# Attention and FFN on one core: later batches in five steps of three score units, three rotating PSUM bank pairs, and a last third of the FFN weights that VectorE holds back

## The chip, the cores and the metric

One core of one Trainium2 chip. The metric is the device time of one execution in microseconds (us); lower is better. A time is the median over the runs of a kernel; each experiment ran in five rounds beside the kernel before, on the same chip. A difference of less than 2% counts as "the same". In the profiles PE is TensorE, ACT ScalarE, DVE VectorE, POOL GpSimd and SP SyncE; L498 is line 498 of the kernel of that profile, so line numbers differ by a few between kernels.

## The reference

Causal attention for 8 batches of 8 heads with 576 queries and 16 "beacon" keys ahead of the 576 keys, then a gated FFN over all 4608 rows:

```python
def _attn_ref(q, k, v, beacon_k, beacon_v):
    B, H, S, D = q.shape                      # 8, 8, 576, 64
    k_all = np.concatenate([beacon_k, k], axis=2)
    v_all = np.concatenate([beacon_v, v], axis=2)
    scores = (1.0 / np.sqrt(D)) * np.matmul(q, k_all.transpose(0, 1, 3, 2))
    ...                                       # causal mask, softmax over the keys
    return np.matmul(a, v_all)

def _moe_ref(x, w_gate, w_val, w_out):        # x: 4608 x 512, FFN width 1536
    gate = np.maximum(x @ w_gate, 0.0)
    return (gate * (x @ w_val)) @ w_out
```

Inputs and outputs are float32; the kernel computes in bf16 with float32 sums.

## The kernel before

The program is written as a list of steps. A step of attention takes two score units (a unit fills up to a pair of PSUM banks with scores), their exponentials on ACT, causal masks on POOL, the weighted sums ("values") of an earlier chunk of queries, and then some FFN products of rows that are finished. Batch 0 and 1 go in an order of their own; batches 2 to 7 are the *later batches*, seven steps of two units each. The FFN of one tile of 512 rows is 12 *slices* (a gate product, its Relu on ACT, a value product, their product hT on DVE) and four *down* products of 12 matmuls.

The eight PSUM banks belong to three pools: two pairs for scores, two banks for FFN products, one each for the values and their row sums.

```python
s_ps = main.enter_context(tc.tile_pool(name="s_ps", bufs=2, space=bass.MemoryType.PSUM))
o_ps = main.enter_context(tc.tile_pool(name="o_ps", bufs=1, space=bass.MemoryType.PSUM))
f_ps = main.enter_context(tc.tile_pool(name="f_ps", bufs=2, space=bass.MemoryType.PSUM))
# ... cut ...
def up(self, nf, c0, c1, spare):                       # one slice
    # ...
    g = f_ps.tile([P, M_TILE], FP32, name="f")          # gate product into g
    # ... 4 matmuls; gs = Relu(g) on ScalarE
    if spare:
        u = s_ps.tile([P, 2, M_TILE], FP32, name="s")[:, 0]
    else:
        u = f_ps.tile([P, M_TILE], FP32, name="f")      # value product into u
    # ... 4 matmuls; hT = gs * u on VectorE
```

The front, that is the work on batches 0 and 1, loads everything that comes later: on POOL's queue the third part of the gate and value weights ("thirds", four loads of 192 KB as the profile counts them) and the output weights (wo, two loads), on SP's queue the tiles of q, k and v, which POOL casts to bf16 and SP then transposes.

```python
for t in range(NKT):
    after(7, lambda t=t: second.load("v", t, t == 0))
for t in range(NKT):
    after(s2 - 1 + t // 2, lambda t=t: second.cast("v", t, pool))
after(s2 - 2, lambda: load_w(wg, moe_w_gate, 1152, 1536))     # thirds
after(s2 - 2, lambda: load_w(wv, moe_w_val, 1152, 1536))
after(s2 - 1, lambda: load_wo(0, 6))                          # output weights
after(s2, lambda: load_wo(6, 12))
# ... cut ...
def fetch(b, s0, late=1):
    for j, u in enumerate(UNITS):                 # k, q, v of tile 0, then of tile 1, ...
        s = s0 + j // 3                           # three loads a step
        at(s, lambda u=u: batches[b].load(*u))
        at(s + late, lambda u=u: batches[b].cast(*u, pool))
        if u[0] != "v":
            at(s + late + 1, lambda u=u: batches[b].turn(*u))   # transpose on SP

fetch(2, s2, 3)
fetch(3, BASE[3] - STEPS - 2, 2)
for b in range(4, B):
    fetch(b, BASE[b] - STEPS)
```

## Time and profile before

| what | value |
|---|---|
| median of 3 runs | 393.25 us (390.98 to 393.74) |
| span of the profiled run | 389.1 us |
| PE busy | 374.1 us, 96% |
| DVE, ACT, POOL busy | 53%, 50%, 33% |
| one later batch (same product to same product) | 40.55 us |
| idle of PE, all waits | 10.0 us, all before 120 us |

The profile of a kernel is read from the bound engine outward: the busy shares and the row of slices say which engine and which stretch matter, the timeline of that engine says what one period costs, and its list of waits says who ended each pause. PE's last pause, and one period, from a down product to the same one of the next batch:

```profile
118.73 0.29 PE L368 MATMUL s<-qT,kT 64*128 64x128 bf16 x4 [0.28 <-DMA qT<-half]
...
146.67 5.35 PE L483 MATMUL f<-wo,hT 128*128 128x512 bf16 x24
...
187.22 5.35 PE L483 MATMUL f<-wo,hT 128*128 128x512 bf16 x24
```

PE shows no pause from 120 us on, so there only PE's own work counts. Before that it pauses for 10.0 us in all, and there what counts is who comes late.

### The profile page before, as it was taken

What the parts mean: (1) busy time and instruction counts of PE and PEld (TensorE: products, weight loads), DVE (VectorE), ACT (ScalarE), POOL (GpSimd) and SP (SyncE); (2) the same over time, 40 slices, a digit from 0 to 9 for tenths busy, and PEclk for the clock granted to TensorE, in tenths of its full rate; (3) what the DMA queues carried; (4) which work ended last, traced back from release to release, by engine and by line L of the source; (5) the groups of instructions that cost most, each with busy time, mean ns of one, the idle gap of its engine ahead of it and who ended that gap; (6) DMA issues with size and microseconds to landing.
All of it is one profiled execution on the core that took longest, in us unless ns stands there. A gap on an engine that the chain in (4) does not pass through costs nothing.

```text
span 389.1 us, 10272 instructions
## 1 busy us (share of the span) xinstructions
PE 374.1 (96%) x4297; PEld 187.4 (48%) x4297; DVE 204.3 (53%) x342; ACT 192.9 (50%) x270; POOL 127.8 (33%) x220
## 2 busy tenths in 40 slices
PE   7889889998999999999999999999999999999995
PEld 3554435543554545545544545445545454444443
DVE  4767456543566566465547653757266635512420
ACT  4763556336555554565546554655466533323321
POOL 1597284334462462253414351435021100000000
PEclk9999989999999999999999999999999999999999
DMA  8999999979996996499449933993300020011002
GB/s 215 215 186 178 200 199 210 166 174 174 215 161 164 188 183 125 115 203 172 101 128 193 182 86 106 197 203 77 98 29 2 2 83 29 0 52 59 0 29 87
DMA packets 148132, 50.44 MB, mean 130 GB/s; under 512 B 133616, under 2 KB 143600, under 8 KB 148080
## 3 DMA queue, kind: packets, MB, share of 16 engines
q1 hardware_dynamic: 139024, 44.48, 57.2%
q0 software_dynamic: 9056, 5.24, 9.8%
q8 instruction: 35, 0.57, 0.7%
q14 instruction: 17, 0.14, 0.1%
HBM read 38.34 MB, written 9.44 MB: 123 GB/s over the span
## 4 chain that ended last, share of the span: by engine, by line
PE 75%; DMA 12%; SPq 6%; POOL 4%; issue 1%; DVE 1%; ACT 0%; POOLq 0%; DVEq 0%
PE f L483 22%; PE f L464 21%; PE s L473 11%; PE f L473 9%; PE ab L418 6%; PE s L368 5%; DMA raw<-in_v_dram 5%; DMA raw<-in_k_dram 2%; PE os L418 2%; SPq L244 2%; DMA wv<-in_moe_w_val_dram 2%; SPq L268 2%; SPq L281 1%; DMA qT<-half 1%; POOL e L384 1%
## 5 line engine op out<-in xcount | busy, mean ns | idle before, releaser
L376 ACT ACTIVATE e<-s 128x1024 bf16<-128x1024 f32 (+2 forms) x112 | 104.9, 963 | 25.3 <-PE s L368 25.3
L464 PE MATMUL f<-xT,wg 128*128 128x512 bf16 x432 | 112.2, 382 | 0.3 <-DMA hwide<-in_k_dram 0.3
L467 ACT ACTIVATE g<-f 128x512 f32<-128x512 f32 x108 | 64.5, 597 | 84.6 <-PE f L464 82.6
L483 PE MATMUL f<-wo,hT 128*128 128x512 bf16 (+1 forms) x444 | 96.7, 374 | 0.0
L384 POOL TENSOR_SCALAR_AFFINE_SELECT e<-e 128x512 bf16<-128x512 bf16 (+2 forms) x80 | 46.8, 597 | 135.6 <-ACT e L376 127.6
L430 DVE RECIPROCAL r<-os 128x80 f32<-128x80 f32 (+2 forms) x43 | 57.6, 1339 | 57.0 <-PE os L418 57.0
L475 DVE TENSOR_TENSOR hT<-g,s 128x512 bf16<-128x512 f32 x60 | 41.2, 687 | 66.4 <-PE s L473 65.3
L473 PEld LDWEIGHTS <-wv 128*128 128x128 bf16 x432 | 42.3, 98 | 53.3 <-issue 3.0
L483 PEld LDWEIGHTS <-hT 128*128 128x128 bf16 x444 | 41.9, 98 | 47.3
L464 PEld LDWEIGHTS <-wg 128*128 128x128 bf16 x432 | 39.6, 98 | 46.8 <-issue 1.7
L473 PE MATMUL s<-xT,wv 128*128 128x512 bf16 x240 | 61.6, 379 | 0.0
L486 ACT COPY ob<-f 128x512 f32<-128x512 f32 (+1 forms) x37 | 21.3, 575 | 73.9 <-PE f L483 71.9
L475 DVE TENSOR_TENSOR hT<-g,f 128x512 bf16<-128x512 f32 x48 | 33.0, 688 | 36.6 <-PE f L473 32.0
L473 PE MATMUL f<-xT,wv 128*128 128x512 bf16 x192 | 49.8, 381 | 0.6 <-DMA wv<-in_moe_w_val_dram 0.4
L263 POOL CAST half<-raw 128x512 bf16<-128x512 f32 (+2 forms) x60 | 37.4, 634 | 31.0 <-DMA raw<-in_k_dram 11.3
L418 PE MATMUL ab<-e,v 128*32 128x80 bf16 (+4 forms) x1320 | 39.3, 233 | 3.8 <-POOL e L384 3.8
L368 PE MATMUL s<-qT,kT 64*128 64x80 bf16 (+3 forms) x704 | 35.8, 235 | 1.8 <-ACT e L376 1.0
L418 PEld LDWEIGHTS <-v 128*32 128x32 bf16 (+1 forms) x1408 | 26.5, 97 | 13.6 <-issue 9.0
L259 POOL CAST v<-raw 128x512 bf16<-128x512 f32 (+1 forms) x40 | 26.5, 664 | 19.3 <-DMA raw<-in_v_dram 19.3
L368 PEld LDWEIGHTS <-kT 64*128 64x128 bf16 x704 | 20.3, 96 | 25.8 <-issue 23.7
L418 PE MATMUL os<-e,ones 128*32 128x240 bf16 (+4 forms) x660 | 32.2, 232 | 0.0
L443 DVE TENSOR_TENSOR xT<-ab,r 128x480 bf16<-128x480 f32 (+2 forms) x45 | 24.9, 554 | 0.8
(66 smaller groups left out, 134.7 us busy)
## 6 DMA issues: line engine op xcount, KB each, us to landing
out_dram<-ob SPq DMA_DIRECT2D x35, 256.0 KB, 2.1
raw<-in_q_dram SPq DMA_DIRECT2D x25, 256.0 KB, 4.8
raw<-in_v_dram SPq DMA_DIRECT2D x24, 256.0 KB, 5.0
raw<-in_k_dram SPq DMA_DIRECT2D x19, 256.0 KB, 4.3
raw<-in_v_dram SPq DMA_DIRECT2D x8, 224.0 KB, 4.2
wo<-in_moe_w_out_dram POOLq DMA_DIRECT2D x2, 768.0 KB, 9.9
raw<-in_k_dram SPq DMA_DIRECT2D x6, 224.0 KB, 4.5
raw<-in_v_dram SPq DMA_DIRECT2D x8, 160.0 KB, 4.3
```

What stands on the lines that cost most here:

```text
L259: copy(self.v[:n, t].rearrange("p (h a d) -> p h a d", a=2, d=C), raw[:n].rearrange("p (h d a) -> p h a d", a=2, d=C))
L263: copy(h[:n], raw[:n])
L368: nc.tensor.matmul(self.s[:, a, c + j * n:c + (j + 1) * n], kT[rows, 2 * g + j, k0:k0 + P], qT[rows, 2 * g + j, q0:q0 + n], start=True, st ...
L376: nc.scalar.activation(e[:, :k * 4 * n].rearrange("p (k a x) -> p a k x", k=k, a=2), self.s[:, :, :k * 2 * n].rearrange("p a (k x) -> p a ...
L384: nc.gpsimd.affine_select(out=cols[:, :, :m], in_=cols[:, :, :m], pattern=[[0, 4], [1, m]], compare_op=ALU.is_ge, fill=0.0, base=base, cha ...
L418: nc.tensor.matmul(o[:, q0 - cq0:q0 - cq0 + n], w, e[:kr, 2 * (hh % 2) + hh // 2], start=(i == 0 and part != 1), stop=(i == self.last), sk ...
L430: nc.vector.reciprocal(self.r[:, :n], self.os[:, :n])
L464: nc.tensor.matmul(g[:, :n], wg[:, ki, nf * P:(nf + 1) * P], x[:, ki], start=(ki == 0), stop=(ki == KM - 1))
L467: nc.scalar.activation(gs[:, :n], g[:, :n], AF.Relu)
L473: nc.tensor.matmul(u[:, :n], wv[:, ki, nf * P:(nf + 1) * P], x[:, ki], start=(ki == 0), stop=(ki == KM - 1))
L475: nc.vector.tensor_mul(self.h[:, nf, c0:c1], gs[:, :n], u[:, :n])
L483: nc.tensor.matmul(o[:, n], self.h[:, nf, ms * P:(ms + 1) * P], wo[:, nf, n], start=(nf == 0), stop=(nf == NF - 1))
```

## The change

The intent: every change of tile shape on PE costs about 0.1 us, so fewer and larger steps (five steps of 3, 3, 3, 3 and 2 units) save some. Three units at a time need three pairs of score banks, so the two score pairs and the two FFN banks become three pairs in one rotation, and FFN products use one bank of a pair. Chunks 0 and 2 of a head group are summed in one go. In the front, DVE writes one element of the last weight third after an FFN product; the load of that third has to wait for it, so that the v tiles of batch 1 get the DMA engines first.

```diff
+SHARES_FIRST, SHARES = (2,) * 7, (3, 3, 3, 3, 2)
-    s_ps = main.enter_context(tc.tile_pool(name="s_ps", bufs=2, ...PSUM))
-    f_ps = main.enter_context(tc.tile_pool(name="f_ps", bufs=2, ...PSUM))
+    # s_ps and f_ps are closed when batch 2 starts, then:
+            pools["p"] = main.enter_context(
+                tc.tile_pool(name="p_ps", bufs=3, space=bass.MemoryType.PSUM))
+    LOADS = ([("k", 0), ("q", 1), ("k", 1), ("q", 2), ("k", 2), ("q", 3), ("k", 3), ("q", 0),
+              ("k", 4), ("q", 4)] + [("v", t) for t in range(NKT)])
+    def bank():
+        return pair()[:, 0] if "p" in pools else f_ps.tile([P, 512], FP32, name="f")
...
-            g = f_ps.tile([P, M_TILE], FP32, name="f")
+            g = bank()
...
-                u = f_ps.tile([P, M_TILE], FP32, name="f")
+                u = bank()
...
+        def load_thirds():
+            nc.vector.memset(wg[:1, 0, 1152:1153], 0.0)
+            load_w(wg, moe_w_gate, 1152, 1536)
+            load_w(wv, moe_w_val, 1152, 1536)
+            for t in range(2, NKT):
+                second.load("v", t, t == 2)
+        after(s2 - 1, load_thirds)
+        # load_wo(0, 6) and load_wo(6, 12) both after(s2, ...), behind the casts of v 0 and 1
...
-        fetch(2, s2, 3)
-        fetch(3, BASE[3] - STEPS - 2, 2)
-        for b in range(4, B):
-            fetch(b, BASE[b] - STEPS)
+        fetch(2, s2 + 1, 2, True)
+        for b in range(3, B):
+            fetch(b, BASE[b] - 5)          # and fetch() goes through LOADS, not UNITS
...
             for j, u in enumerate(units):
-                u.qk()
+                if len(units) > 2 and not chunks and j == 0:
+                    u.qk(o_ps.tile([P, 2, 512], FP32, name="o"))
+                else:
+                    u.qk()
...
+            if len(units) > 2:
+                for u in units[1:]:
+                    u.exp()
```

The cuts: the new order of units, the sums of two chunks in one tile, the wider tiles for their reciprocals, and bookkeeping.

## The prediction

> **What bounds the kernel now.** I read the page's busy shares and slices first, then the table of stretches, then TensorE's (PE) timeline through one later batch, with ScalarE's (ACT) and VectorE's (DVE) beside it, and last PE's waits.
>
> ```profile
> PE 374.1 (96%) x4297; PEld 187.4 (48%) x4297; DVE 204.3 (53%) x342; ACT 192.9 (50%) x270; POOL 127.8 (33%) x220
> ...
> PE   7889889998999999999999999999999999999995
> ...
> PEclk9999989999999999999999999999999999999999
> ```
>
> PE is busy 96%, every other engine about half. From the stretches (start:end, length, busy us and count of each engine):
>
> ```profile
> 40.00:60.00 20.00, 16.95 (x194) 8.20 (x193) 10.55 (x13) 11.80 (x17) 9.72 (x17) 0.91 1.16 200
> ...
> 80.00:100.00 20.00, 18.67 (x134) 8.54 (x133) 8.88 (x14) 10.87 (x15) 7.44 (x13) 1.00 0.88 171
> ...
> 160.00:180.00 20.00, 20.00 (x211) 9.79 (x196) 12.65 (x19) 12.21 (x17) 9.17 (x16) 1.00 1.05 180
> ...
> 200.00:220.00 20.00, 20.00 (x246) 10.03 (x241) 12.19 (x18) 12.77 (x18) 8.59 (x16) 1.00 1.00 184
> ```
>
> From 120 us until the last matmuls PE has no idle time. The same down projection starts at 146.67, 187.22 and 227.77 in the PE timeline: 40.55 us a batch. So from 120 us on only PE's own time counts; before that PE idles about 10 us. One step of a later batch, by start and length (the length contains the drain, so the next start is what counts):
>
> ```profile
> 162.76 1.03 PE L473 MATMUL f<-xT,wv 128*128 128x512 bf16 x4
> 163.72 0.61 PE L368 MATMUL s<-qT,kT 64*128 64x256 bf16 x8
> 164.26 0.39 PE L418 MATMUL ab<-e,v 128*32 128x240 bf16 x8
> 164.47 0.28 PE L418 MATMUL os<-e,ones 128*32 128x240 bf16 x4
> 164.58 0.28 PE L418 MATMUL ab<-e,v 128*32 128x128 bf16 x8
> 164.69 0.23 PE L418 MATMUL os<-e,ones 128*32 128x128 bf16 x4
> 164.85 1.04 PE L464 MATMUL f<-xT,wg 128*128 128x512 bf16 x4
> 165.72 1.03 PE L473 MATMUL f<-xT,wv 128*128 128x512 bf16 x4
> ```
>
> Four 512-column matmuls take 0.86 to 0.87 us (164.85 to 165.72). The group before the scores takes 0.96 (162.76 to 163.72): 0.10 more. Eight score matmuls (two at a time, 1024 columns each, 0.43 us at 2.4 columns per ns) take 0.54: 0.11 more. The values (4416 columns, four at a time, 0.46 us) take 0.59: 0.13 more. So a step with values pays 0.34 us for three changes of tile shape; one without values pays 0.10 + 0.11 = 0.21.
>
> Two stalls lie in the front, both on POOL's masks, the first followed by a half-speed gate product (1.68 us to the next start, against 0.86):
>
> ```profile
> 50.22 0.39 PE L418 MATMUL ab<-e,v 128*32 128x240 bf16 x8 [2.15 <-POOL e L384]
> 50.42 0.29 PE L418 MATMUL os<-e,ones 128*32 128x240 bf16 x4
> 51.00 0.41 PE L418 MATMUL ab<-e,v 128*32 128x128 bf16 x8 [0.29 <-POOL e L384]
> 51.17 0.35 PE L418 MATMUL os<-e,ones 128*32 128x128 bf16 x4
> 51.45 0.61 PE L368 MATMUL s<-qT,kT 64*128 64x256 bf16 x4
> 51.99 1.89 PE L464 MATMUL f<-xT,wg 128*128 128x512 bf16 x4
> ```
>
> The other is 1.33 us at 95.03, for the same reason.
>
> **What the Trainium skill says.** "TensorEngine Tiling (Array Packing)", Tiling Modes, Key Properties: changing the tiling mode, not just the tile, drains TensorE. The trace agrees: 0.10 to 0.13 us at each change. "TensorE: Matmul & The Clock Gate", Part 1: after an idle window of some 3.4 us the array clock falls to half until a busy window passes. The trace agrees in size (1.68 against 0.86) though the idle before it was only 2.15 + 0.29 us in one piece and more. "PSUM — Partial Sum Buffer", Specifications: eight banks of 512 fp32 per partition. Both kernels use all eight, before as 2 x 2 for scores, 2 for FFN products and 2 for values, after as 3 pairs plus one pair. "DMA: Bandwidth & Descriptors", Issuing engines are not separate DMA queues: all transfers share 16 engines. The trace agrees: from 52 to 56 us POOL's queue moved 0.59 MB and SP's 0.12 MB, and an SP load issued there took 11.4 us to land.
>
> **The change part by part.** The order of instructions of the changed kernel has the same matmuls, but 36 fewer stretches of one tile shape: 12 fewer each of scores, values and FFN.
>
> 1. *Fewer steps: gain.* A later batch goes from six steps with values and one without (6 x 0.34 + 0.21 = 2.25 us) to four and one (1.57): 0.68 us a batch, 4.1 us for six batches.
>
> 2. *Three rotating pairs: new waits.* Each score unit, gate, value or down product now takes the next of three pairs, so each waits for the reader of the third product before it. Before, FFN products rotated in their own banks, and PE never waited. Durations from the rows: exp of 1024 columns 1.02 us, a second follows 0.93 after the first; relu 0.60; hT product 0.69; output copy 0.59. Reader starts after PE's last issue: exp 0.22 (170.14 + 0.21 to 170.57), hT product 0.27 (170.31 against 170.04), copy 0.21. I take 0.06 us from a reader's end to PE's next start. Counted from the end of the FFN before:
> - Step 0 (two downs before it): its third unit needs the pair of the second down, copied at 0.21 + 0.59 + 0.06 = 0.86. PE is there at 0.10 + 0.21 + 0.21 = 0.52. Wait 0.34.
> - Step 1 (no values, first unit in the values' pair): the first value product needs the pair of the second unit. The first exp, behind the copy, starts at 0.69, the second ends at 0.69 + 0.93 + 0.97 = 2.59, PE may go at 2.65. PE arrives at 0.10 + 0.61 (three units) + 0.11 + 0.86 = 1.68. Wait 0.97.
> - Step 2: its third unit needs the pair of the last value product, free at 0.27 + 0.69 + 0.06 = 1.02; PE is there at 0.10 + 0.13 + 0.21 = 0.44. Wait 0.58.
> - Step 3: the same with 0.52 for 0.44. Wait 0.50.
> - Step 4 has two units and no such wait.
>
> Sum 2.39 us a batch against 0.68 gained: +1.7 us a batch, a period of 42.25 us. Five batches (3 to 7): +8.5 us. Batch 2 has short steps: waits of about 0.8, 0.2, 0.6, 0.6, 0.5 and 0.3 (values waiting for DVE's scaling), 3.0 - 0.7 = +2.3 us.
>
> 3. *Merged chunks.* One 320-column reciprocal replaces one of 240 and one of 80: 2.16 us (line through 657 ns at 80 and 1758 at 256) for 2.31, and fewer minimum and maximum instructions. DVE is 53% busy; nothing on the path.
>
> 4. *New unit order and load order for batch 2 on.* The 1.33 us stall near 95 us and a 0.28 us one at 118.73 go, because values come two steps after their masks: -1.6 us.
>
> 5. *Last weight third held, wo later.* The memset sits in DVE's order behind an hT product that ends near 44.5 us. POOL waits there, issues four loads (0.71 us each) to 47.5, casts two v tiles to 48.8, masks at 49.35: the values start at 49.4 instead of 50.22, their second part at 50.0 instead of 51.0, and with only 1.3 us idle the half clock (about 1.2 us lost) should not come: some 2 us gained by 54 us. But both halves of wo are now issued behind those masks, at 50.5 to 52.3 instead of 48.7 and 52.6, into engines that still carry the thirds. At 0.15 MB per us (0.59 MB in 4 us) the 1.57 MB run from 53 to 63.5 or 64; the second half is needed 1.3 us into the first down, at about 61.5. That is 2 to 2.5 us of wait. SP's loads creep meanwhile, and POOL stands at batch 2's casts ahead of masks that batch 1 needs: 1 to 2 us more, perhaps a half clock. Net of the front: +2 us, uncertain by 2.5.
>
> Sum: 8.5 + 2.3 - 1.6 + 2 = +11.2 us if all holds. I shade it to +9.75, since the front is the weakest part and small waits can overlap: 403.0 us.
>
> **The rivals.** (a) *The switches decide*: the waits of part 2 hide, PE stays full, 4.1 us of drains and 1.6 + 2 us of front go: about 385.5 us. For it: PE has shown no wait in 270 us. Against: in step 1 two exps of about 1 us each must end before a product that PE reaches in 1.68 us; and in the built program that product's pair is the second unit's. (b) *Drains and waits cancel*: if the consumers start sooner than I read, waits of 1.0 a batch leave 0.3 us a batch, and the front decides: 392 to 396 us. (c) *A longer front*: the wo wait brings the half clock and batch 3's loads, now spread over only five short steps, come late: 408 us. For it: DMA was above 0.9 busy in the slices to 120 us. (d) *DVE becomes the bound* through the 2.16 us reciprocal: it would delay the first hT product of a step; against it, the pair it holds is needed only three products later.
>
> **Range and chances.** The steady part is +8.5 + 2.3 with perhaps 2 us of error, the front -2 to +5. So 403.0 us, 8 in 10 within 396 to 409. Slower by 2% begins at 401.1 us: 0.64 for slower, 0.31 for within 2%, 0.05 for faster.
>
> **What would show it.** In the changed profile: the starts of the same down 42.2 us apart in batches 4 to 6 (40.55 before); PE waiting for the score exps (about 1 us, once a batch), for hT (about 0.5, twice) and for the output copy (0.3, once); PE below 20.0 in 20 us in the stretches after 120; about 0.34 us per step of drains as before; the values of batch 1 starting near 49.4 us; a PE wait for wo near 62 us; no wait for POOL near 95. A period under 40.5 us would prove part 2 wrong; PE full again from 120 us on would prove rival (a); no wait at the first down would prove part 5 wrong.

## More of the kernel before

The experiments ran in four groups (e1 to e4, e5 to e8, e9 to e11, e12), each on another chip, so across groups the ratios are compared, not the times.

## The result, and the profile after

The changed kernel took 406.41 us (405.55 to 407.61, four runs) against 392.75 us (four runs) for the kernel before beside it: ratio 1.0355, 95% interval 1.0307 to 1.0402, slower. A ratio here is the mean time of one kernel's fast runs over the mean of the other's fast runs of the same rounds, so it is not quite the ratio of the medians.

The page of the changed kernel, busy time and slices:

```profile
PE 369.7 (91%) x4252; PEld 189.0 (47%) x4297; DVE 198.6 (49%) x307; ACT 191.3 (47%) x270; POOL 124.2 (31%) x222
...
PE   6879787899896999989998999999999999999995
...
PEclk9799998999999999999999999999999999999999
```

The span is 404.7 us for 389.1. PE's busy time reads lower than before (369.7 for 374.1), but 45 of its 4297 matmul records are missing from this trace (x4252; e10, with all of them, has 375.4), so that is no gain. In the later batches four matmuls still take 0.86 to 0.87 us (173.38 to 174.25 below): they did not get slower, PE waits. In the stretches (start:end, length, then busy time and number of each engine, PE first) it is no longer at 20.00 in the later batches:

```profile
160.00:180.00 20.00, 18.86 (x202) 9.31 (x203) 6.50 (x10) 10.10 (x15) 6.46 (x12) 1.00 0.68 161
```

Whom PE waited for (sum, times, longest):

```profile
PE p L381 <- DVE hT L500: 4.6, 13, 0.5
PE p L498 <- ACT e L389: 4.3, 5, 1.0
PE o L438 <- POOL e L397: 3.6, 3, 1.4
PE p L381 <- DMA qT<-half: 3.1, 1, 3.1
PE f L508 <- DMA wo<-in_moe_w_out_dram: 2.5, 1, 2.5
```

The tile `p` is a rotating pair. The first two lines are the later batches, the other three the front and batch 3. All waits of PE sum to 27.7 us (some of the missing records count as pauses in it), against 10.0 before. One later batch in PE's timeline (start, length, operation, number; in brackets the pause shown ahead of it and who ended it):

```profile
170.85 0.40 PE L381 MATMUL o<-qT,kT 64*128 64x128 bf16 x8
...
171.60 0.82 PE L489 MATMUL p<-xT,wg 128*128 128x512 bf16 x3
173.38 1.02 PE L498 MATMUL p<-xT,wv 128*128 128x512 bf16 x4 [0.96 <-ACT e L389]
174.25 1.02 PE L489 MATMUL p<-xT,wg 128*128 128x512 bf16 x4
...
179.52 0.54 PE L381 MATMUL p<-qT,kT 64*128 64x80 bf16 x12
180.43 0.39 PE L381 MATMUL p<-qT,kT 64*128 64x256 bf16 x4 [0.38 <-DVE hT L500]
...
182.02 1.04 PE L489 MATMUL p<-xT,wg 128*128 128x512 bf16 x3
...
215.47 1.02 PE L498 MATMUL p<-xT,wv 128*128 128x512 bf16 x4 [0.96 <-ACT e L389]
```

From 173.38 to 215.47 a batch takes 42.09 us, where it took 40.55. In step 1 (170.85) a value product waits until an exponential has read the pair that it is to fill; ACT's timeline shows which:

```profile
171.44 1.03 ACT L389 ACTIVATE e<-o 128x1024 bf16<-128x1024 f32 x1
172.35 1.84 ACT L389 ACTIVATE e<-p 128x960 bf16<-128x960 f32 x2
```

The first exponential reads the output pair, which PE does not need back for a whole step; the one PE waits for stands second. In step 2 (179.52) the third unit waits for the hT product that reads its pair. Two warnings on the brackets. The group at 171.60 has three records of four: one matmul is missing from the trace, so the 0.96 holds the missing 0.21 or so as well; where all four records are there (several experiments below) the same wait reads 0.74. And the 0.38 is too small, since the end of a matmul is a modelled time: the Trainium skill, "Perfetto Trace Analysis", Tensor Engine Instruction, says that the profiler estimates a matmul's end from its size. The starts tell more, and they are used further down.

The front and batch 3 in PE's timeline:

```profile
53.23 0.60 PE L498 MATMUL f<-xT,wv 128*128 128x512 bf16 x2 [0.66 <-DMA wv<-in_moe_w_val_dram]
...
66.33 2.04 PE L508 MATMUL f<-wo,hT 128*128 128x512 bf16 x6 [2.54 <-DMA wo<-in_moe_w_out_dram]
...
130.10 0.39 PE L381 MATMUL p<-qT,kT 64*128 64x80 bf16 x12 [3.08 <-DMA qT<-half]
...
131.29 1.03 PE L498 MATMUL p<-xT,wv 128*128 128x512 bf16 x4
```

POOL's timeline around the write of DVE that holds the thirds back:

```profile
45.67 1.41 POOL L341 DMA_DIRECT2D wg<-in_moe_w_gate_dram  x2 [7.49 <-DVE wg L693]
...
51.41 1.67 POOL L359 DMA_DIRECT2D wo<-in_moe_w_out_dram  x2
```

POOL stands 7.49 us at DVE's write, issues the thirds, and the output weights only at 51.41. The thirds are then late for the products that need them (0.66, and 0.80 at 54.63), the output weights 2.54 us late for the first down product; the six matmuls behind that wait take 2.04 us at reduced clock (0.91 of full in the stretch from 60 to 80 us), where six take 1.46 or 1.47 in other runs. At 79.31 a mask is 1.18 us late. The last down product ahead of batch 2 starts at 79.75, against 73.75 before. In batch 3 the transpose of the last q tile comes 3.08 us late (130.10); it was issued only in that batch's own step 0.

Where the 15.6 us between the two profiled runs lie: 6.0 before the last down product of the front, of which 1.4 were there at the first FFN product (27.99 us against 26.56); the experiments have that product at 26.7 to 28.4, so these 1.4 are the run's. Five later batches of +1.54 make 7.7. Batch 3's late transpose adds 2.35, not the whole 3.08: behind it the first value product of step 1 waits for no exponential any more (131.29), and from step 1 to the next batch's step 1 are 44.44 us (126.41 to 170.85) where the other later batches take 42.09. That is 16.05; batch 2 and the end give back 0.45.

### The profile page after: what moved, and what is told of

Read it like the earlier page. It is cut to its first block, busy times and chain, and to the rows that moved or that the text cites. A ratio compares the mean times of both kernels' runs of the same rounds, so it can differ in the third digit from the quotient of the medians.

```text
span 404.7 us, 10190 instructions
## 1 busy us (share of the span) xinstructions
PE 369.7 (91%) x4252; PEld 189.0 (47%) x4297; DVE 198.6 (49%) x307; ACT 191.3 (47%) x270; POOL 124.2 (31%) x222
## 4 chain that ended last, share of the span: by engine, by line
PE 69%; DMA 10%; SPq 7%; ACT 4%; issue 3%; DVE 3%; POOL 3%; DVEq 0%; ACTq 0%; POOLq 0%
PE p L498 18%; PE p L508 18%; PE p L489 17%; PE o L438 6%; SPq L247 3%; DMA raw<-in_v_dram 3%; PE f L489 2%; DMA raw<-in_k_dram 2%; DVE hT L500 2%; PE p L381 2%; ACT e L389 2%; DMA wv<-in_moe_w_val_dram 2%; PE s L498 1%; SPq L271 1%; ACT ob L511 1%
## 5 line engine op out<-in xcount | busy, mean ns | idle before, releaser
L500 DVE TENSOR_TENSOR hT<-g,p 128x512 bf16<-128x512 f32 x89 | 60.9, 684 | 108.5 <-PE p L498 79.6
L498 PE MATMUL p<-xT,wv 128*128 128x512 bf16 x355 | 91.3, 379 | 4.4 <-ACT e L389 4.3
L492 ACT ACTIVATE g<-p 128x512 f32<-128x512 f32 x89 | 53.3, 599 | 80.2 <-PE p L489 78.5
L489 PE MATMUL p<-xT,wg 128*128 128x512 bf16 x335 | 89.4, 379 | 0.9
L508 PE MATMUL p<-wo,hT 128*128 128x512 bf16 (+1 forms) x383 | 84.6, 373 | 0.8 <-issue 0.2
L451 DVE RECIPROCAL r<-o 128x256 f32<-128x256 f32 (+3 forms) x31 | 55.8, 1799 | 54.4 <-PE o L438 54.4
L389 ACT ACTIVATE e<-p 128x1024 bf16<-128x1024 f32 (+2 forms) x77 | 68.9, 961 | 12.6 <-PE p L381 12.6
L438 PE MATMUL o<-e,v 128*32 128x80 bf16 (+4 forms) x1320 | 38.4, 234 | 4.3 <-POOL e L397 3.6
L389 ACT ACTIVATE e<-s 128x1024 bf16<-128x1024 f32 (+2 forms) x28 | 25.7, 962 | 8.7 <-PE s L381 8.7
L489 PE MATMUL f<-xT,wg 128*128 128x512 bf16 x73 | 19.5, 380 | 0.5 <-DMA hwide<-in_k_dram 0.3
```

The source lines that it names most:

```text
L389: nc.scalar.activation(e[:, :k * 4 * n].rearrange("p (k a x) -> p a k x", k=k, a=2), self.s[:, :, :k * 2 * n].rearrange("p a (k x) -> p a ...
L438: nc.tensor.matmul(o[:, q0 - cq0:q0 - cq0 + n], w, e[:kr, 2 * (hh % 2) + hh // 2], start=(x == 0 and i == 0 and part != 1), stop=stop, ski ...
L451: nc.vector.reciprocal(self.r[:, :self.n], self.os[:, :self.n])
L489: nc.tensor.matmul(g[:, :n], wg[:, ki, nf * P:(nf + 1) * P], x[:, ki], start=(ki == 0), stop=(ki == KM - 1))
L492: nc.scalar.activation(gs[:, :n], g[:, :n], AF.Relu)
L498: nc.tensor.matmul(u[:, :n], wv[:, ki, nf * P:(nf + 1) * P], x[:, ki], start=(ki == 0), stop=(ki == KM - 1))
```

## The experiments

All outputs are right.

| label | edit, in a few words | time, us | ratio to before | 95% interval |
|---|---|---|---|---|
| (changed kernel) | | 406.41 | 1.0355 | 1.0307 to 1.0402 |
| e1_pair_shared | gate and value product share a pair | 486.12 | 1.2433 | 1.2389 to 1.2476 |
| e2_third_late | third unit behind the values | 402.33 | 1.0269 | 1.0243 to 1.0294 |
| e3_old_front | old loads, new order of batch 2's tiles | 410.58 | 1.0495 | 1.0467 to 1.0523 |
| e4_front_only | kernel before with the new front | 395.13 | 1.0092 | 1.0070 to 1.0114 |
| e5_third_in_o | third unit in the output pair | 405.57 | 1.0364 | 1.0320 to 1.0409 |
| e6_batch3_earlier | batch 3 fetched earlier | 404.20 | 1.0326 | 1.0280 to 1.0371 |
| e7_early_hold | DVE's write earlier | 405.47 | 1.0337 | 1.0302 to 1.0373 |
| e8_all_four | e2, e5, e6 and e7 together | 395.26 | 1.0066 | 1.0037 to 1.0096 |
| e9_whole_old_front | old loads, old order of batch 2's tiles | 404.27 | 1.0290 | 1.0266 to 1.0314 |
| e10_exp_behind_relu | e2, and the exponentials in another order | 399.62 | 1.0201 | 1.0174 to 1.0228 |
| e11_combined | e6, e9 and e10 together | 391.33 | 0.9976 | 0.9961 to 0.9991 |
| e12_tuned | e11 with three small moves | 394.01 | 1.0040 | 1.0011 to 1.0068 |

### e1_pair_shared: fewer allocations in the rotation

```diff
-            g = bank()
+            gu = pair() if "p" in pools else None
+            g = bank() if gu is None else gu[:, 0]
...
-                u = bank()
+                u = bank() if gu is None else gu[:, 1]
```

> Edit: in the changed kernel, gate and value product of one slice share one PSUM pair (gate in its first bank, value in its second) instead of taking a pair each. Theory (three rotating pairs bring new waits): the 0.96 us wait of step 1's first value product for the second unit's exponential goes, the two short waits of the third units (0.38 and 0.30) stay; the period of a batch falls from 42.08 to about 41.1 us and the time by about 5 us to 401. Rival (the five-step order itself, with its merged 320-wide sums and longer exponentials, is what costs): the period stays at 42.0 to 42.2 and the time within 1.5 us of the changed kernel's 406.4.

Measured: 486.12 us. Both theories were far off. From the list of waits:

```profile
PE p L499 <- ACT g L493: 69.1, 89, 2.1
```

One slice in PE's timeline:

```profile
254.61 1.03 PE L490 MATMUL p<-xT,wg 128*128 128x512 bf16 x4
256.32 1.02 PE L499 MATMUL p<-xT,wv 128*128 128x512 bf16 x4 [0.69 <-ACT g L493]
```

The wait for the exponential is gone from the list, but now every value product waits for the Relu of its own gate product, though that reads the other bank of the pair. A slice takes 2.57 us from gate to gate (254.61 to 257.18) instead of 1.73; 89 such slices make 75 us. Whether it is the chip or the program's bookkeeping that treats the pair as one, this run does not tell; either way a pair is one buffer for waiting. The experiment says nothing on step 1's wait, so e5 and e10 take it up.

### e2_third_late: third unit behind the values

```diff
+            late = units[2:] if chunks else []
-            for j, u in enumerate(units):
+            for j, u in enumerate(units[:len(units) - len(late)]):
...
+            for u in late:
+                u.qk()
             if len(units) > 2:
                 for u in units[1:]:
                     u.exp()
```

> Edit: in the changed kernel, where a step has weighted sums to do, the scores of its third unit come after these sums rather than before. Theory (rotation waits): the third unit's scores no longer wait for the last hT product or for the output copy (0.38, 0.30 and some 0.5 us in step 0), at the cost of one more change of tile shape in each of three steps (0.11 us each); the period falls from 42.08 to about 41.3 us, the time by about 4 us to 402.5; the 0.96 us wait of step 1 stays. Rival (these waits are only moved behind the sums, or the later exponential makes a new wait): period 42.0 or more, time 406 to 408.

Measured: 402.33 us, a period of 41.03 (the wait of step 1 at 173.98 and 215.01). The waits of the third units are gone, the 0.74 in step 1 stays. The theory holds for mechanism and time; the period fell a little further than said, because the true losses were larger than the brackets (see below).

### e3_old_front: the front of before, not quite

```diff
-        fetch(2, s2 + 1, 2, True)
+        fetch(2, s2, 3)
 # and the loads and casts of v, thirds and wo as in the kernel before
```

> Edit: the changed kernel with the front of the kernel before: last weight thirds, v loads, output weights and batch 2's fetch issued and cast where the kernel before has them; steps and PSUM pairs as changed. Theory (the new front costs 4 to 5 us through the late output weights, the half clock after their wait, and batch 3's loads): the first down product of tile 0 waits for nothing, batch 2 starts near 89 instead of 94.3, and the time falls by 4 to 7 us to 400 to 402. Rival (the front costs nothing, all of the 13.7 us lies in the steady batches): 405 to 408.

Measured: 410.58 us, slower than the changed kernel; the expectation failed. The wait for the output weights is gone, but a mask of batch 1 is 4.51 us late (79.09). POOL's timeline says why:

```profile
75.01 1.17 POOL L266 CAST half<-raw 128x512 bf16<-128x512 f32 x2 [6.99 <-DMA kT<-half]
...
78.57 0.47 POOL L397 TENSOR_SCALAR_AFFINE_SELECT e<-e 128x320 bf16<-128x320 bf16 x1
```

The changed kernel loads all ten k and q tiles of batch 2 before any v. Their casts need one of six half-precision buffers each, and a buffer comes free only when its transpose has run; so POOL stands 6.99 us at a cast, with the mask behind it. The twelve matmuls behind that mask's wait then take 4.88 us (79.42) instead of 2.76: the clock was reduced there (0.81 of full from 80 to 90 us). That load order is a part of the change that I had kept. e9 undoes it too.

### e4_front_only: the kernel before with the new front

```diff
 # kernel before: v loads split, thirds behind DVE's write, wo behind the casts of v 0 and 1,
 # as in the change; seven steps, old pools and old fetches stay
```

> Edit: the kernel before with only the new front (v loads split, last weight thirds held behind VectorE's write, output weights later); its seven steps and its PSUM pools stay. Theory (the front alone costs 4 to 5 us): 396 to 398 us, with a wait of about 2.5 us of the first down product for the output weights and the half clock behind it. Rival (front is neutral): 391.5 to 394.

Measured: 395.13 us, ratio 1.0092, or 3.6 us. The first mask of batch 1 is 1.40 us late instead of 2.15, but then the output weights are 1.26 us late and a mask 2.88 us late (at 69.91, behind a cast of batch 2's v that waited for its load). So the new front costs by itself, a little less than said, and most of it is the masks rather than the output weights.

### e5_third_in_o: which unit gets the output pair

```diff
-                if len(units) > 2 and not chunks and j == 0:
+                if len(units) > 2 and not chunks and j == 2:
```

> Edit: in the changed kernel's step without weighted sums (step 1 of a batch) the third unit's scores go to the output pair instead of the first unit's. Then the first value product of that step takes the rotating pair of the first unit, whose exponential ends first. Theory (the pair rotation makes the wait): the wait of that value product for an exponential, 0.74 to 0.96 us per batch, shrinks to 0.2 or less, the period falls from 42.09 to 41.3 or 41.4 us and the time by 4 to 5 us, to about 402. Rival (ScalarE is late as a whole: the wait passes on to the next gate product, which takes the second unit's pair): period 41.9 to 42.1, time 405 to 407.

Measured: 405.57 us; the period is 41.72, between the two theories. From PE's timeline:

```profile
174.27 1.02 PE L498 MATMUL p<-xT,wv 128*128 128x512 bf16 x4 [0.33 <-ACT g L492]
```

The first value product no longer waits, but the second takes the pair of the first gate, whose Relu stands behind three exponentials on ACT (it starts at 173.59). The rotation passed the wait on by two products. By time alone this run is not told apart from the changed kernel (its profile shows 0.37 us a batch, some 2 us).

### e6_batch3_earlier: batch 3 fetched two steps earlier

```diff
-        for b in range(3, B):
+        fetch(3, BASE[3] - 7, 2)
+        for b in range(4, B):
             fetch(b, BASE[b] - 5)
```

> Edit: in the changed kernel, batch 3's loads start two steps earlier and its casts lie two steps behind them, as in the kernel before. Theory (five short steps of batch 2 leave the fetch of batch 3 no time): the 3.08 us wait of batch 3's step 1 for a transposed q goes and the time falls by about 3 us, to 403.5. Rival (DMA is saturated there, and the wait or another one for data stays): wait of over 1 us left there or in batch 2's start, time 405 to 407.

Measured: 404.20 us. In the profile the wait of 3.08 us shrank to 0.46 (at 125.80), as the theory says. The expected 3 us were too many: with the transpose in time, step 1's value product waits for the exponential in batch 3 too (0.33 at 127.27), and of the 3.08 only 2.35 were extra. The times alone are inconclusive: the intervals of this run and of the changed kernel overlap.

### e7_early_hold: DVE's write one product earlier

```diff
-            nc.vector.memset(wg[:1, 0, 1152:1153], 0.0)      # in load_thirds, after step s2 - 1
...
-        mid[s2 - 1] = lambda: turn_two(second, 0, s_ps)
+        def turn_and_free():
+            turn_two(second, 0, s_ps)
+            nc.vector.memset(wg[:1, 0, 1152:1153], 0.0)
+        mid[s2 - 1] = turn_and_free
```

> Edit: in the changed kernel the one-element write of VectorE that holds the last weight thirds back stands one FFN product earlier on VectorE, some 1.8 us sooner. Theory (the thirds, the masks and the output weights all queue behind this write on GpSimd): the waits for the third of the value weights (0.66 and 0.80) and the wait of the first weighted sums (1.42) go to under 0.3 each, the wait of the first down product for the output weights shrinks from 2.54 to about 0.7, and the time falls by 2 to 4 us to 402.5 to 404.5. Rival (the transfers, not their issue, set these waits: the same bytes go through the same queues): the thirds and output weights land hardly earlier, waits of 2 us or more in sum stay, time 405 to 407.

Measured: 405.47 us; the time is the rival's. The waits that were to go did shrink: the first mask's from 1.42 to none shown, the output weights' from 2.54 to 0.64. But the thirds are now 1.75 us late in one piece instead of 0.66 and 0.80, and the masks later on take up the rest:

```profile
68.94 0.40 PE L438 MATMUL o<-e,v 128*32 128x256 bf16 x8 [2.37 <-POOL e L397]
```

with another 1.48 at 78.15. The five waits of the changed kernel's front sum to 1.42 + 0.66 + 0.80 + 2.54 + 1.18 = 6.6 us, those of this run to 1.75 + 0.64 + 2.37 + 1.48 = 6.2. Here the order of issue decided who waits, hardly for how long in sum.

### e8_all_four: do the repairs add up?

```diff
 # the edits of e2, e5, e6 and e7 together
```

> Edit: the changed kernel with the four repairs together: third unit after the weighted sums, output pair for the third unit in the step without sums, batch 3 fetched two steps earlier, early hold. Theory (the costs are separate waits of the chain that ends last, so that they add): period 40.2 to 40.4 us, below the 40.55 of the kernel before; the time falls by 4.1 + 4.5 + 3 + 3 to about 391 to 393, level with the kernel before. Rival (repairs hide each other, or the masks on GpSimd take the place): 395 or more.

Measured: 395.26 us; the period is 40.66. Both expectations were missed (40.2 to 40.4, and 391 to 393); the time is the rival's 395, and for the reason it named, waits in the front. The period is what e2 and e5 took off alone: 42.09 - 1.06 - 0.37 = 40.66, so these costs add to the hundredth. It is not below 40.55, since e5 left 0.33. The front stayed long: 3.47 us of wait for the output weights, 1.55 for a mask.

### e9_whole_old_front: the front of before, wholly

```diff
-        fetch(2, s2 + 1, 2, True)
+        fetch(2, s2, 3)
...
-            for j, u in enumerate(LOADS):
+            for j, u in enumerate(UNITS if b == 2 else LOADS):
 # and the loads and casts of v, thirds and wo as in the kernel before
```

> Edit: as the old front of the third experiment, and besides batch 2's loads in the old order (k, q, v of one tile in turn, instead of all k and q first). Theory (in the third experiment ten k and q casts in a row waited on GpSimd for half-precision buffers and kept the masks behind them waiting 4.5 us; the old front with the old order has none of this): the last down product before batch 2 starts near 74 instead of 79.4, and the time falls to 400 to 402, 5 to 6 us below the changed kernel. Rival (the front of the changed kernel is no worse than the old one once the steps are five): 405 or more.

Measured: 404.27 us, 0.65% of the kernel before's time, or 2.6 us, under the changed kernel; the intervals overlap by a hair. The last down product of the front starts at 75.15 instead of 79.42 in e3, and no mask after the first is late. So the load order was the fault in e3. The gain is half of what I expected: in this run the first mask of batch 1 is 3.62 us late (2.15 in the kernel before), and batch 3's transpose is again late, by 3.60.

### e10_exp_behind_relu: the order on ScalarE

```diff
+            behind_relu = len(units) > 2 and not chunks and b > 2
             if units and s > 0:
-                units[0].exp()
+                if not behind_relu:
+                    units[0].exp()
...
-            other = units[1:] if len(units) == 2 else []
+            other = units[1:] if len(units) == 2 else units[:1] if behind_relu else []
 # and the edit of e2
```

> Edit: third unit after the sums (as in the second experiment), and in the step without sums the exponential of the first unit, which lies in the output pair that nobody asks for, comes behind the first gate's Relu on ScalarE; the two units in rotating pairs go first. Theory (the wait is one of the order on ScalarE: a rotating pair is freed late because another exponential goes first): no wait of over 0.25 us in step 1, period 40.3 to 40.4 instead of 41.03, time 4 us below the second experiment's 402.3, so about 398.5. Rival (ScalarE simply has too much to do there, as the 0.33 us that stayed in the fifth experiment hints): a wait of 0.3 or more stays, period 40.6 to 41.0, time 400 or more.

Measured: 399.62 us (397.37 to 401.58). PE's timeline, with no bracket from batch 3's step 2 to the end:

```profile
169.26 0.40 PE L381 MATMUL o<-qT,kT 64*128 64x128 bf16 x8
...
171.79 1.03 PE L489 MATMUL p<-xT,wg 128*128 128x512 bf16 x4
...
177.06 0.54 PE L381 MATMUL p<-qT,kT 64*128 64x80 bf16 x12
...
217.23 0.54 PE L381 MATMUL p<-qT,kT 64*128 64x80 bf16 x12
```

The period is 40.17 us (177.06 to 217.23), below the 40.55 of the kernel before. ACT has the same work as in the changed kernel; only the exponential that nobody waits for moved behind the first Relu. So the wait was one of order, and the rival falls. The time is a microsecond over what was said; its runs spread over 4 us, and its profiled run (span 395.7) is the fastest of them.

### e11_combined

```diff
 # the edits of e6, e9 and e10 together
```

> Edit: the two edits of this call's other runs together, and batch 3 fetched two steps earlier. Theory (costs add): front 5 to 6 us, steady batches 1.7 us each over five and a half batches, batch 3's load 3 us: 406.4 minus 17 to 19 is 387.5 to 390, so 0.5 to 1 per cent below the kernel before. Rival (something of the changed structure costs that no wait shows, or a wait in batch 2 or 3 comes back): 393 or more.

Measured: 391.33 us, ratio 0.9976 (0.9961 to 0.9991): a quarter of a per cent faster than the kernel before, so "the same", and 15 us below the changed kernel. It missed the expected 387.5 to 390. The period is 40.17 again; what it lost lies ahead of batch 3: 2.86 us for batch 1's first mask, 1.24 us at batch 2's first scores (the profile names nobody for it; two transposes were issued at 87.84 and 89.17, shortly before), 0.62 for an exponential in batch 2 and 0.90 for the output pair there.

### e12_tuned

```diff
-        after(s2 - 1, lambda: load_wo(0, 6))
+        mid[s2] = lambda: load_wo(0, 6)
...
-        fetch(3, BASE[3] - 7, 2)
+        fetch(3, BASE[3] - 6)
...
-            behind_relu = len(units) > 2 and not chunks and b > 2
+            behind_relu = len(units) > 2 and not chunks and b >= 2
```

> Edit: the combined version of the eleventh experiment, with three small moves more: batch 1's first mask goes ahead of the issue of the first half of the output weights on GpSimd; batch 3 is fetched one step earlier than in the changed kernel instead of two; the exponential behind the Relu also in batch 2. Theory (what the eleventh still loses lies in three waits of the front: 2.86 for batch 1's first mask, 1.24 at batch 2's start behind the transposes that now queue with batch 3's loads, 0.62 for an exponential in batch 2): these shrink by about 0.8, 1.2 and 0.6, the steady period stays at 40.17, the time is 388.5 to 390, 0.6 to 1 per cent below the kernel before. Rival (the first loads fill the DMA engines, so that each wait taken away comes back at the next transfer): 390.5 to 392.5, as the eleventh.

Measured: 394.01 us, ratio 1.0040: slower than e11. The three waits did shrink (2.86 to 1.63, 1.24 to 0.37, 0.62 to none), but three others came, all for masks: 1.15 at 52.63, 0.74 at 102.37 and 2.22 at 118.91. The last one stands behind casts of v that waited for their loads. The rival was right in kind; the time was 1.5 us worse even than it said. Like e7, it moved the waits of the front, and this time at a loss.

## Why the prediction was right or wrong

The prediction said 403.0 us, slower more likely than not; it was 406.4, slower. By its own steps:

1. **Fewer steps: right.** It put the period without waits at 39.87 us. e10 shows no wait of PE from batch 3's step 2 on and has three of the six changes of tile shape less: 40.17 for 40.55, 0.38 us for three, where the prediction has 0.34. The other three are taken off by the prediction's own 0.11 us each, which no run shows alone: 40.17 - 0.33 = 39.84. "No wait" is good to some 0.1 us: in the step without values the value product starts 0.92 us after its gate product in e10 (170.01 to 170.93) and 0.97 in the kernel before (170.68 to 171.65), elsewhere 0.86 to 0.87.

2. **The new waits of the rotation: right, in each term.** The starts give the true loss of a step: from its first score to the first product behind its scores and values, in the changed kernel against e10. Step 0: 163.34 to 165.57, 2.23, against 1.99 (202.15 to 204.14). Step 1, up to the second gate: 3.40 against 2.53 (169.26 to 171.79). Step 2: 2.50 (179.52 to 182.02) against 2.06. Step 3: 2.36 (189.04 to 191.40) against 1.99. Where e10 has the extra change (all but step 1), 0.11 is added to the difference.

| step | predicted wait | loss by the starts | in the bracket |
|---|---|---|---|
| 0, third unit, output copy | 0.34 | 0.35 | none shown |
| 1, first value product, exponential | 0.97 | 0.87 | 0.96 (0.74 with all records) |
| 2, third unit, hT | 0.58 | 0.55 | 0.38 |
| 3, third unit, hT | 0.50 | 0.48 | 0.30 |
| sum | 2.39 | 2.25 | |

   That 39.84 + 2.25 gives the measured 42.09 is no check, since the differences to e10 went in; what is tested is the share of each step. e2 checks it apart: it took 1.06 off the batch and added three changes, so the third units had cost 1.39 (1.06 + 0.33), where the table has 1.38. The prediction had a period of 42.25. Over five batches that is 7.7 us for the 8.5 predicted. e10, with e2's edit in it, shows that these waits are the cause: it takes 1.92 us off the batch by order alone, with the same work. Batch 2 was put at +2.3 - 1.6; its shown waits sum to 1.95 of the 3.0 expected, and what batch 2 and the end did together is -0.45 by subtraction, which no experiment isolates.

3. **Merged chunks: right, as far as seen.** No wait for a reciprocal shows in batches 3 to 7, and with the same reciprocals e10 keeps PE full there. In batch 2 the values wait 0.31 us for DVE's scaling (predicted 0.3; 0.90 in e2 and e10). Rival (d) falls.

4. **The stalls at 95 and 118.7 us: right for the first, misread for the second.** PE waits for no mask near 95 us any more (e4, with the old steps, keeps that wait: 1.45 us at 99.07). But the stall at 118.73 was never one of masks: its line, shown with the profile before, names a transposed q (of batch 3, whose scores begin there). A wait of that kind did not go: batch 3 of the changed kernel has the 3.08 us at 130.10. Read rightly, the line was a sign of what the sum left out.

5. **The front: right in its parts, too small in sum.** The first mask's wait fell from 2.15 to 1.42 and no half clock followed. The last was luck of the run: behind the same wait (1.42 or 1.43) the clock was 1.00 from 50 to 60 us in the changed kernel, e5 and e6, but 0.83 in e10, where the next gate product took 1.89 us for 1.04. Then the output weights came 2.54 us late (2 to 2.5 predicted), with reduced clock behind; the late mask (1.18) was named too. The term that was mis-sized is the gain: "some 2 us gained by 54 us" did not count that the held thirds themselves would be late (0.66 + 0.80). The net of +2 was +4.6 in the profile at the last down product (6.0 less the 1.4 of the run's start), just beyond the "uncertain by 2.5"; by the times it is 3.6 in e4 and 2.6 in e9, within it.

What the sum left out altogether is batch 3's load: a wait of 3.08 us, 2.35 us net, which rival (c) named and which I had not put into the number. e6 shows that fetching earlier takes the wait away. (What it said for itself, DMA above 0.9 busy in the slices to 120 us, is not quite so: two of these slices are at 8 and 7 tenths.) Rival (c) thus came true for half: the reduced clock and the late loads came, and the result lies between 403 and its 408. Rival (a) is wrong for the kernel as changed, whose waits do not hide; e10 shows the gain of the fewer steps once they are gone, and it is 0.38 us a batch. Rival (b) was wrong: the readers of the pairs start as late as was read off.

Left open: the timed runs of kernels with the changed front spread over 6.0 us in e6 and 4.2 in e10, but over 2.1 in the changed kernel itself. The reduced clock would do that, since it follows the waits of the front and of batch 3 in some runs and not in others (from 130 to 140 us it is 0.88 in e10 and 0.83 in e2, 1.00 in the changed kernel), but no run shows it alone.

## What to carry to other kernels

Before pooling PSUM buffers that had pools of their own into one rotation, write down for each product who reads the buffer three (or however many) allocations back, and when that reader ends; the waits came out within 0.1 us each by this sum. Where such a wait shows, look at the order on the reading engine first: moving one exponential that nobody waited for took away 0.86 us a batch (e2 against e10) without any new buffer. Where the first loads fill the DMA engines, reordering them moves the waits more than it removes them, and an in-order engine that both casts loaded tiles and masks scores makes the masks wait for loads that have nothing to do with them.

## What the Trainium skill lacked or had wrong

- "TensorEngine Tiling (Array Packing)", Key Properties, says that changing the tiling mode drains TensorE, not what that costs. The runs: 0.10 to 0.13 us a change, and three fewer changes a batch gave 0.38 us (40.17 in e10 against 40.55).
- "Perfetto Trace Analysis", Matmuls, advises rotating independent groups through different PSUM banks so that the reading of one overlaps the next. Different banks were not enough: with gate and value product in the two banks of one allocated pair, each value product waited for the Relu of the other bank, 2.57 us a slice instead of 1.73 (e1; whether chip or program makes the pair one is open). And a rotation of three pairs cost 2.25 us a batch until the order of the readers fitted.
- "Perfetto Trace Analysis", Tensor Engine Instruction, says that a matmul's end is estimated; it does not say what that does to pauses. The pauses shown were 0.38 and 0.30 us where the starts show losses of 0.55 and 0.48.
- "TensorE: Matmul & The Clock Gate", Part 1, gives an idle window of some 3.4 us before the clock falls. In the changed kernel the matmuls behind a wait of 2.54 us ran slower already (2.04 us for six instead of 1.47), in e10 those behind 1.43 us (0.83 of full from 50 to 60 us), and in the changed kernel those behind 1.42 did not (1.00): the length of one wait does not tell.
- No page that I read has the cost of the casts on GpSimd for the masks behind them: waits of 1.2 to 4.5 us of TensorE, from casts that waited up to 6.99 us for a buffer.
